# A spectral filter and two token MLPs on one core: the first layers of three units ahead of the first second layer

## The chip, the cores and the metric

The kernel runs on one core of a Trainium2 chip. The metric is the device time of one execution in microseconds; below, a time is a median of several runs where it says so, and the profile is one execution of its own. The engines are named as in the profile: PE (TensorE), DVE (VectorE), ACT (ScalarE), POOL (GpSimd) and SP, which here only issues transfers.

## What is computed

The input is `x`, four sequences of 3136 tokens of 256 numbers, in fp32.

```python
X = np.fft.rfft(x, axis=1)                       # a filter along the sequence
y = np.fft.irfft(X * (filt_r + 1j * filt_i), n=3136, axis=1)

u = y + np.real(np.fft.fft(np.fft.fft(y, axis=1), axis=2))   # mixing over both axes
un = (u - mean(u)) / np.sqrt(var(u) + 1e-6)
u = u + np.maximum(un @ w_ch1, 0.0) @ w_ch2      # first layer: weights 1a, 2a

xn = (u - mean(u)) / np.sqrt(var(u) + 1e-6) * g_ln
out = u + np.maximum(xn @ v_ch1, 0.0) @ v_ch2    # second layer: weights 1b, 2b
```

Means and variances are taken over the 256 numbers of a token; `w_ch1` and `v_ch1` have 256 x 1024 numbers, the other two 1024 x 256. The weights are in float64.

## The kernel before

**Transforms.** The sequence of 3136 is split as 64 x 49. For each of the four sequences `b`, `over_p(b)` does the transform over 64 and writes its result `g` to DRAM; `over_q(b)` reads it back, does the transform over 49, the filter and the way back, and writes the rows `v` to DRAM and a part `zt` to SBUF. For `b = 0` this is the opening of the program, up to some 85 us; for the others the generators are called in small turns in between the work of the MLPs. Of `over_p(1)`, ten turns run in the opening and six are put into steps by the table `P1`; `over_q(1)` is put into steps by `MID`, `OPQ` and `PAIRS`.

**Units.** The tokens are cut into 25 units of 512 (the last has 256). A unit is prepared by `prep_ticks(U)` in eight turns: two build `zs` and split the loaded rows `vr` into a high and a low half; two make the tokens `u` (26 matmuls, L216 and L549; ACT copies one half to `uo`, DVE adds and subtracts, L554 and L556); one takes statistics (`bs`, `mv`, `rs`, with a power on POOL at L598); one normalizes into four tiles `xn` (DVE L602); two transpose on PE (L611) and split into `xth` (ACT) and `xtl` (DVE, L220). For the second layer `ln_ticks(U, 1)` does the last four turns again, with L614 for the low half. Tables (`PREP1`, `PREPS`, `PREPN`, `LN0`, `LN`) say in which steps the turns stand.

**Steps.** A layer of a unit is a block of eight steps. Each step `m` has a w1 product of six matmuls of 512 columns (L682, into PSUM), from which ACT makes `hh` (L687) and DVE the low half `hl` (L688), and a w2 product (L705) of eight matmuls with `hh` and four with `hl`, 256 columns each. In the program's order the w1 product of step i + 1 stands ahead of all that is put into step i, and the w2 product of step i behind it. All numbers are split in a high and a low half, so that three passes give fp32. In this kernel the blocks follow each other as unit 0 first layer, unit 1 first, unit 0 second, unit 2 first, unit 1 second, and so on; the order is written out by hand, each engine runs its instructions in that order.

**Conversion of the weights.** Four weights of 4 chunks each, 16 in all, come as float64 words and are turned into a high and a low fp32 half by integer work. `conv_ticks` does it in ticks, as a pipeline: a full tick has, for the newest chunk, three DVE instructions on the words (L665 to L667), for the chunk before two ACT instructions (L658, L659), for the one before that two on DVE (L651, L653) and a product on POOL (L655), and for the oldest the split: the high half on ACT (L219) and the difference on POOL (L220). Three chunks of 1a are done in the opening (`NA`); the 13 others are run by the letters `c` of `DURING` and `AFTER` and then, one tick a step, by the steps in `CONV`: here 0, 1, 3, 6, 9, 11, 12, 14, 15, 17 and 19. On DVE a full tick is thus five instructions in a row, and one that is put into a step stands between two `hl`.

**The turn into the steps.** `AFTER` is a string that is run when `over_q(0)` is done: `p` is a turn of unit 0's preparation, `f` one of `over_p(1)`, `c` one of the conversion and `s` a split of constants. Unit 0's rows are read back from DRAM in this stretch.

## Time and profile before

| | us |
|---|---|
| median of 3 runs | 1429.06 |
| lowest and highest | 1428.6, 1431.17 |
| the profiled execution, its own time | 1427.74 |
| its span in the profile | 1425.9 |
| PE busy in it | 1384.6 |
| DVE, ACT, POOL busy in it | 885.6, 622.7, 408.3 |

A row of a timeline gives the start in us from the span's beginning, the length, the engine, the line and the tiles as out<-in; the number in brackets is how long the engine had stood idle ahead of it, and what it was waiting for. In a table of stretches an engine's number is its busy time in that stretch, with the number of its instructions. The granted clock (PEclk) is a share of full speed; 1.00 is 2.4 GHz and 0.50 is 1.2 GHz. Work of a line by groups: how many, busy time in all, mean of one in ns.

### The profile page before, as it was taken

To read this page: it belongs to the slowest core of one execution; us is meant where nothing else is said; L and a number is where in the kernel's file an instruction comes from. 1 tells how busy PE (TensorE), PEld (TensorE's weight loads), DVE (VectorE), ACT (ScalarE), POOL (GpSimd) and SP (SyncE) were. 2 spreads that over 40 slices of the span, in tenths; PEclk is the share of its full clock that TensorE was granted. 3 is DMA by queue.
4 is the path that set the end of the run, shared out by engine and by line. 5 is a ranking of instruction groups with operands and counts; after the bars stand their busy time and mean duration, and the time that the engine had idled before them with its cause. 6 is when DMAs were issued, how large, how long until landed. Compare 5 with 4: busy or idle time off the path is not lost.

```text
span 1425.9 us, 22918 instructions
## 1 busy us (share of the span) xinstructions
PE 1384.6 (97%) x8835; PEld 1221.6 (86%) x8835; DVE 885.6 (62%) x1814; ACT 622.7 (44%) x1350; POOL 408.3 (29%) x361
## 2 busy tenths in 40 slices
PE   4978999999999999999999999999999999999998
PEld 2437899888989999898999998898999999999998
DVE  2779977777554775767545666667555555555453
ACT  4755545645444544545344355445333233323222
POOL 1635534535231333434032244334100010100000
PEclk7988999999999999999999999999999999999999
DMA  9973332422233313312233233131000000000000
GB/s 325 316 272 108 102 99 83 141 78 85 77 115 124 97 49 114 109 48 68 68 103 118 77 90 114 42 114 62 19 30 30 31 1 31 30 15 16 30 15 23
DMA packets 65981, 123.66 MB, mean 87 GB/s; under 512 B 6096, under 2 KB 32848, under 8 KB 65872
## 3 DMA queue, kind: packets, MB, share of 16 engines
q1 hardware_dynamic: 49920, 99.00, 21.6%
q10 hardware_dynamic: 15952, 23.20, 5.0%
q8 instruction: 69, 1.13, 0.3%
q14 instruction: 40, 0.33, 0.1%
HBM read 83.12 MB, written 39.06 MB: 86 GB/s over the span
## 4 chain that ended last, share of the span: by engine, by line
PE 88%; DVE 5%; DMA 1%; issue 1%; ACT 0%; POOL 0%; ACTq 0%; POOLq 0%; DVEq 0%
PE ps L705 37%; PE ps L682 36%; PE ps L216 11%; PE ps L611 3%; DMA vd<-vst 1%; PE ps L439 1%; DVE we L651 1%; DVE wm L653 0%; DVE hl L688 0%; DVE wm L666 0%; DVE ww L667 0%; DVE xn L602 0%; PE ps L549 0%; POOL rs L598 0%; PE ps L302 0%
## 5 line engine op out<-in xcount | busy, mean ns | idle before, releaser
L687 ACT ACTIVATE hh<-ps 128x512 fp32r<-128x512 f32 (+1 forms) x400 | 235.4, 589 | 689.3 <-PE ps L682 666.9
L688 DVE SCALAR_TENSOR_TENSOR hl<-ps,hh 128x512 fp32r<-128x512 f32 (+1 forms) x400 | 271.7, 680 | 424.5 <-ACT hh L687 423.3
L682 PE MATMUL ps<-xth,w1a 128*128 128x512 f32 (+1 forms) x800 | 247.0, 391 | 0.0
L682 PE MATMUL ps<-xth,w1b 128*128 128x512 f32 (+1 forms) x800 | 243.7, 386 | 0.0
L705 PE MATMUL ps<-w2a,hh 128*128 128x256 f32 x1568 | 221.3, 283 | 2.0 <-ACT hh L687 2.0
L705 PE MATMUL ps<-w2b,hh 128*128 128x256 f32 x1568 | 218.3, 281 | 0.0
L705 PEld LDWEIGHTS ps<-w2b,hh 128*128 128x128 f32 x1568 | 206.2, 188 | 10.5
L705 PEld LDWEIGHTS ps<-w2a,hh 128*128 128x128 f32 x1568 | 205.3, 189 | 10.9 <-ACT hh L687 2.4
L598 POOL TENSOR_TENSOR rs<-rs,mhalf 128x4 f32<-128x4 f32 (+1 forms) x51 | 50.4, 988 | 413.8 <-DVE rs L597 405.6
L682 PE MATMUL ps<-xtl,w1a 128*128 128x512 f32 (+1 forms) x400 | 156.4, 391 | 0.0
L682 PE MATMUL ps<-xtl,w1b 128*128 128x512 f32 (+1 forms) x400 | 155.7, 389 | 0.0
L682 PEld LDWEIGHTS ps<-xth,w1a 128*128 128x128 f32 x800 | 136.8, 190 | 18.0 <-ACT xth L219 0.5
L682 PEld LDWEIGHTS ps<-xth,w1b 128*128 128x128 f32 x800 | 135.2, 188 | 16.5
L705 PE MATMUL ps<-w2a,hl 128*128 128x256 f32 x784 | 123.4, 279 | 3.8 <-DVE hl L688 3.8
L705 PE MATMUL ps<-w2b,hl 128*128 128x256 f32 x784 | 122.0, 277 | 0.1
L422 POOL TENSOR_TENSOR y<-y,t 128x512 f32<-128x512 f32 (+1 forms) x67 | 87.2, 1302 | 99.8 <-DVE t L420 85.7
L705 PEld LDWEIGHTS ps<-w2a,hl 128*128 128x128 f32 x784 | 104.9, 189 | 4.3 <-DVE hl L688 4.3
L705 PEld LDWEIGHTS ps<-w2b,hl 128*128 128x128 f32 x784 | 103.9, 188 | 0.3 <-DVE hl L688 0.3
L220 POOL TENSOR_TENSOR sl<-gr,sh 98x512 fp32r<-98x512 f32 x48 | 63.3, 1318 | 109.7 <-ACT sh L219 107.8
L220 POOL TENSOR_TENSOR sl<-y,sh 128x512 fp32r<-128x512 f32 (+1 forms) x51 | 67.2, 1317 | 79.9 <-issue 59.1
L682 PEld LDWEIGHTS ps<-xtl,w1a 128*128 128x128 f32 x400 | 75.8, 190 | 15.1
L682 PEld LDWEIGHTS ps<-xtl,w1b 128*128 128x128 f32 x400 | 75.3, 188 | 14.4
(115 smaller groups left out, 2040.6 us busy)
## 6 DMA issues: line engine op xcount, KB each, us to landing
fc<-in_ff SPq DMA_DIRECT2D x61, 512.0 KB
vd<-vst ACTq DMA_DIRECT2D x64, 200.0 KB
gr<-gd SPq DMA_DIRECT2D x64, 196.0 KB
xr<-in_x SPq DMA_DIRECT2D x48, 256.0 KB
vr<-vd SPq DMA_DIRECT2D x48, 256.0 KB
out<-u SPq DMA_DIRECT2D x24, 512.0 KB
gd<-gst ACTq DMA_DIRECT2D x28, 256.0 KB
gd<-gst SPq DMA_DIRECT2D x20, 256.0 KB
```

The costliest lines, as they stand in the source:

```text
L216: nc.tensor.matmul(out=o, lhsT=lhs[a], rhs=rhs[b], start=start and i == 0, stop=stop and i == 2)
L220: (lo_eng or nc.vector).tensor_tensor(out=lo, in0=src, in1=f32(hi), op=ALU.subtract)
L422: (nc.gpsimd if b or t < n - 1 else nc.vector).tensor_tensor(out=y[:, :nk], in0=y[:, :nk], in1=t2[:, :nk], op=ALU.add)
L439: nc.tensor.transpose(zp[:, a].rearrange("p t k -> p (t k)"), z[:, a], ident)
L598: nc.gpsimd.tensor_tensor(out=rs[:, tl], in0=rs[:, tl], in1=mhalf[:, tl], op=ALU.pow)
L611: nc.tensor.transpose(ps[:, t * 128:t * 128 + 128], xs[t][:, k * 128:k * 128 + 128], ident)
L651: nc.vector.scalar_tensor_tensor(out=p, in0=w[:, :, 1], scalar=-0x80000000, in1=p, op0=ALU.bitwise_and, op1=ALU.bitwise_or)
L682: nc.tensor.matmul(out=ps[:, :n], lhsT=w[:, a, k, m * 128:m * 128 + 128], rhs=xt[s][:, k, :n], start=i == 0, stop=i == 5)
L687: nc.scalar.activation(out=h[:, :n], in_=ps[:, :n], func=ACTF.Relu)
L688: nc.vector.scalar_tensor_tensor(out=l[:, :n], in0=ps[:, :n], scalar=0.0, in1=f32(h[:, :n]), op0=ALU.max, op1=ALU.subtract)
L705: nc.tensor.matmul(out=o[:, t % 2], lhsT=a[:, t * 128:t * 128 + 128], rhs=w[:, b, m], start=m == 0 and i == 0 and t % 2 == 0, stop=m == 7 ...
```

## The change

The blocks now begin with the first layers of units 0, 1 and 2 (24 steps), then the second layers of units 0 and 1, and from there on alternate as before. So unit 2's first layer is in steps 16 to 23 instead of 24 to 31 and is prepared by `PREP1` in steps 8 to 14; unit 3 has a table of its own (`PREP3`). The second layers' normalizations are counted back from the block that needs them. The chunks are converted in another order: of 1a and 1b those that the first four w1 products need come first, and the first chunk of 2a ahead of the last of 1a; the assertion in `w1_step` asks only for the two chunks that a product reads. One `c` leaves `AFTER`: the one ahead of the two turns that make unit 0's tokens; another turn of `over_p(1)` moves between unit 0's two transposing turns. The conversion takes steps 0, 1, 3, 5, 8, 10, 12, 14, 16, 18, 20 and 22; the six turns of `over_p(1)` steps 4, 7, 9, 11, 13 and 15; `over_q(1)` starts four steps later and gets one more pair of steps in 16.

```diff
+CHUNKS = {"1": (0, 1024, 512, 1536), "2": (0, 512, 1024, 1536)}
-AFTER = "ppcfspfcppfpfppfpppc"
-CONV = (0, 1, 3, 6, 9, 11, 12, 14, 15, 17, 19, 20, 21, 22, 23, 24, 25, 26, 27, 28)
-P1 = (2, 3, 4, 5, 7, 8, 9, 10, 10)
-OPQ = (2, 4)
-MID = 16
+AFTER = "ppcfspfppfpfpfpppc"
+CONV = (0, 1, 3, 5, 8, 10, 12, 14, 16, 18, 20, 22, 26, 27, 28)
+P1 = (4, 7, 9, 11, 13, 15, 17, 19, 20)
+OPQ = (3, 5)
+MID = 20
+PREP3 = (2, 3, 10, 11, 11, 12, 13, 14)
-LN0 = (8, 10, 12, 12)
-LN = (12, 13, 16, 19)
+LN0 = (-12, -9, -7, -5)
+LN = (-12, -11, -8, -5)
...
-            chunks += [(words, n, a) for a in range(0, 2048, 512)]
+            chunks += [(words, n, a) for a in CHUNKS[n[0]]]
         chunks = chunks[first:last]
+        if first:
+            chunks[:2] = chunks[1::-1]
...
-                conv_done.add((names[(i + first) // 4], (i + first) % 4))
+                conv_done.add((name, a // 512))
...
-        assert all(("1" + "ab"[layer], j) in conv_done for j in range(4)), (U, layer, m)
+        assert all(("1" + "ab"[layer], j + m // 4) in conv_done for j in (0, 2)), (U, layer, m)
...
-        blocks = [(0, 0)]
-        for U in range(1, NU + 1):
+        blocks = [(0, 0), (1, 0), (2, 0), (0, 1), (1, 1)]
+        for U in range(3, NU + 1):
             blocks += [(U, 0), (U - 1, 1)]
...
-                for w in (PREPS if V % 6 else PREPN) if U else PREP1:
+                if V == 3:
+                    s = index[V, 0] - 16
+                for w in PREP1 if V < 3 else PREP3 if V == 3 else PREPS if V % 6 else PREPN:
                     put(s + w, it)
...
-                call(s + 1 + new if U else -1, load_v, V)
+                call(s + 1 + new if V > 2 else s - 1, load_v, V)
...
-                e = index[U + 1, 0]
-                for w in [s + v for v in LN] if U else [e - 8 + w for w in LN0]:
-                    put(w, it)
+                for w in LN if U else LN0:
+                    put(index[U, 1] + w, it)
...
-            for each in range(1, len(PAIRS) + 1):
+            pr = PAIRS + [(7, 9)] if b == 1 else PAIRS
+            for each in range(1, len(pr) + 1):
```

Line numbers of the changed kernel are two to seven higher than those of the kernel before (L651 becomes L655, L688 becomes L692).

**DVE, from the loading of unit 0's rows to its normalization.** Before: the last instruction of one tick, a whole tick, then the sum `u`.

```order
L667 TENSOR_SCALAR ww<-ww 128x512
L651 SCALAR_TENSOR_TENSOR we<-ww,we 128x512
L653 SCALAR_TENSOR_TENSOR we<-ww,we 128x512
L665 TENSOR_SCALAR we<-ww 128x512
L666 TENSOR_SCALAR we<-ww 128x512
L667 TENSOR_SCALAR ww<-ww 128x512
L554 TENSOR_TENSOR u<-ps,uo 128x256
L556 TENSOR_TENSOR u<-ps,uo 128x256
L594 BN_STATS bs<-u 128x6 x2
```

The same place now:

```order
L671 TENSOR_SCALAR ww<-ww 128x512
L556 TENSOR_TENSOR u<-ps,uo 128x256
L558 TENSOR_TENSOR u<-ps,uo 128x256
L596 BN_STATS bs<-u 128x6 x2
L598 BN_AGGR mv<-bs 128x2 x2
```

The tick between the two is gone from here.

**DVE, unit 1's normalization in steps 4 to 6.** Before: `xn`, an `hl`, the low half `xtl` of the transposed tokens, then a tick.

```order
L597 TENSOR_SCALAR rs<-mv 128x4
L688 SCALAR_TENSOR_TENSOR hl<-ps,hh 128x512
L602 TENSOR_SCALAR xn<-u,mv,rs 128x256 x4
L688 SCALAR_TENSOR_TENSOR hl<-ps,hh 128x512
L220 TENSOR_TENSOR xtl<-ps,xth 128x512 x2
L651 SCALAR_TENSOR_TENSOR we<-ww,we 128x512
L653 SCALAR_TENSOR_TENSOR wm<-ww,wm 128x512
```

The same place now:

```order
L599 TENSOR_SCALAR rs<-mv 128x4
L692 SCALAR_TENSOR_TENSOR hl<-ps,hh 128x512
L604 TENSOR_SCALAR xn<-u,mv,rs 128x256 x4
L655 SCALAR_TENSOR_TENSOR we<-ww,we 128x512
L657 SCALAR_TENSOR_TENSOR wm<-ww,wm 128x512
L669 TENSOR_SCALAR we<-ww 128x512
L670 TENSOR_SCALAR wm<-ww 128x512
L671 TENSOR_SCALAR ww<-ww 128x512
L692 SCALAR_TENSOR_TENSOR hl<-ps,hh 128x512
L222 TENSOR_TENSOR xtl<-ps,xth 128x512 x2
```

The tick of step 5 stands between `xn` and `xtl`.

**DVE, unit 2's statistics and normalization.** Before (in steps 16 to 19, for a layer that begins in step 24):

```order
L594 BN_STATS bs<-u 128x6 x4
L596 BN_AGGR mv<-bs 128x2 x4
L597 TENSOR_SCALAR rs<-mv 128x4
L688 SCALAR_TENSOR_TENSOR hl<-ps,hh 128x512
L602 TENSOR_SCALAR xn<-u,mv,rs 128x256 x4
```

The same place now (in steps 12 and 13, for a layer that begins in step 16); the second set of statistics is unit 0's for its second layer.

```order
L596 BN_STATS bs<-u 128x6 x4
L598 BN_AGGR mv<-bs 128x2 x4
L599 TENSOR_SCALAR rs<-mv 128x4
L596 BN_STATS bs<-u 128x6 x4
L598 BN_AGGR mv<-bs 128x2 x4
L599 TENSOR_SCALAR rs<-mv 128x4
L655 SCALAR_TENSOR_TENSOR we<-ww,we 128x512
L657 SCALAR_TENSOR_TENSOR wm<-ww,wm 128x512
L669 TENSOR_SCALAR we<-ww 128x512
L670 TENSOR_SCALAR wm<-ww 128x512
L671 TENSOR_SCALAR ww<-ww 128x512
L692 SCALAR_TENSOR_TENSOR hl<-ps,hh 128x512
```

The four `xn` of unit 2 follow that `hl`.

## Rows read from the trace of the kernel before

**Rows 1.** The page, busy time of the engines over the span.

```profile
PE 1384.6 (97%) x8835; PEld 1221.6 (86%) x8835; DVE 885.6 (62%) x1814; ACT 622.7 (44%) x1350; POOL 408.3 (29%) x361
```

**Rows 2.** Table of stretches: length, then PE, PEld, DVE, ACT, POOL busy, clock, DMA.

```profile
93.00:109.00 16.00, 9.79 (x28) 6.35 (x29) 13.60 (x31) 5.93 (x12) 5.25 (x6) 0.79 0.62 220
109.00:142.60 33.60, 28.48 (x165) 25.04 (x165) 30.96 (x49) 18.45 (x38) 20.35 (x18) 0.90 0.31 101
142.60:173.00 30.40, 27.22 (x177) 24.16 (x176) 29.60 (x52) 16.38 (x33) 17.59 (x13) 0.99 0.36 114
173.00:198.00 25.00, 24.89 (x167) 22.57 (x166) 22.91 (x51) 10.55 (x20) 11.82 (x10) 1.00 0.13 41
198.00:400.00 202.00, 202.00 (x1317) 181.35 (x1316) 134.53 (x271) 105.53 (x243) 83.93 (x71) 1.00 0.33 102
```

**Rows 3.** Timeline of PE, the four longest waits from 95 us on.

```profile
100.93 0.56 PE L611 MATMUL ps<-ctail,xn 128*128 128x128 f32 x2 [3.94 <-DVE xn L602]
...
119.64 1.22 PE L705 MATMUL ps<-w2a,hl 128*128 128x256 f32 x4 [2.58 <-DVE hl L688]
...
138.71 0.30 PE L611 MATMUL ps<-ctail,xn 128*128 128x128 f32 x1 [2.21 <-DVE xn L602]
...
170.43 1.19 PE L705 MATMUL ps<-w2a,hh 128*128 128x256 f32 x8 [2.01 <-ACT hh L687]
```

**Rows 4.** Table of stretches again, one stretch of half clock.

```profile
119.20:122.40 3.20, 2.76 (x9) 2.38 (x10) 3.20 (x6) 1.32 (x3) 1.37 (x2) 0.50 0.00 0
```

**Rows 5.** DVE from 93 to 178 us by line, the five instructions of a tick.

```profile
L651 DVE SCALAR_TENSOR_TENSOR we<-ww,we 128x512 int32<-128x512 int32 x11 | 13.1, 1189 | 0.0
...
L666 DVE TENSOR_SCALAR wm<-ww 128x512 int32<-128x512 int32 x9 | 11.4, 1269 | 0.0
L667 DVE TENSOR_SCALAR ww<-ww 128x512 int32<-128x512 int32 x11 | 10.2, 929 | 0.0
L653 DVE SCALAR_TENSOR_TENSOR wm<-ww,wm 128x512 f32<-128x512 int32 x7 | 7.0, 994 | 0.0
...
L665 DVE TENSOR_SCALAR we<-ww 128x512 int32<-128x512 int32 x10 | 5.3, 527 | 0.0
```

**Rows 6.** Timelines of DVE and POOL: the longest tick and the shortest.

```profile
113.22 0.67 DVE L651 SCALAR_TENSOR_TENSOR we<-ww,we 128x512 int32<-128x512 int32 x1
...
114.23 1.63 POOL L220 TENSOR_TENSOR w2a<-we,w2a 128x512 fp32r<-128x512 f32 x1
...
114.62 1.53 DVE L665 TENSOR_SCALAR we<-ww 128x512 int32<-128x512 int32 x1
...
118.91 0.68 DVE L688 SCALAR_TENSOR_TENSOR hl<-ps,hh 128x512 fp32r<-128x512 f32 x1
...
161.78 0.67 DVE L651 SCALAR_TENSOR_TENSOR we<-ww,we 128x512 int32<-128x512 int32 x1
...
164.00 0.67 DVE L688 SCALAR_TENSOR_TENSOR hl<-ps,hh 128x512 fp32r<-128x512 f32 x1
```

**Rows 7.** Timeline of all engines around unit 0's sum.

```profile
93.34 1.78 DVE L651 SCALAR_TENSOR_TENSOR we<-ww,we 128x512 int32<-128x512 int32 x1
94.02 0.38 ACT L553 ACTIVATE uo<-ps 128x256 f32<-128x256 f32 x1 [0.59 <-PE ps L302]
...
97.72 0.41 DVE L554 TENSOR_TENSOR u<-ps,uo 128x256 f32<-128x256 f32 x1
```

**Rows 8.** Timeline of DVE, unit 1's normalization and the second low half.

```profile
137.22 2.72 DVE L602 TENSOR_SCALAR xn<-u,mv,rs 128x256 f32<-128x256 f32 x4 [0.53 <-POOL rs L598]
...
141.99 0.69 DVE L220 TENSOR_TENSOR xtl<-ps,xth 128x512 fp32r<-128x512 f32 x1 [0.16 <-ACT xth L219]
```

**Rows 9.** The chain that ended last: one w1 and one w2 product at full pace.

```profile
190.00 1.40 PE ps L682 x6
191.40 1.39 PE ps L705 x12
```

**Rows 10.** Timeline of DVE, the statistics of one unit.

```profile
182.05 1.39 DVE L594 BATCH_NORM_STATS2 bs<-u 128x6 f32<-128x256 f32 x4
```

More of the change, by code (lines that the diff above doesn't have):

```diff
@@ L850, in spectral_mlp_kernel @@
             if U < NU:
-                e = index[U + 1, 0]
-                for w in [s + v for v in LN] if U else [e - 8 + w for w in LN0]:
-                    put(w, it)
+                for w in LN if U else LN0:
+                    put(index[U, 1] + w, it)
             else:
                 for w in (9, 10, 12, 13):
-                    put(s + w, it)
+                    put(index[U, 0] + w, it)
         conv_at = CONV[:16 - NA + LAG + 1 - nc_]
@@ L875, in spectral_mlp_kernel @@
                 put(w, q)
-            for each in range(1, len(PAIRS) + 1):
+            pr = PAIRS + [(7, 9)] if b == 1 else PAIRS
+            for each in range(1, len(pr) + 1):
                 slots = []
                 for base in range(-8, end, 16):
-                    for h in sorted(PAIRS[:each]):
+                    for h in sorted(pr[:each]):
                         if base + h[0] > mid + (4 if b > 1 else OPQ[1] + 1) and base + h[1] < end:
```

## The prediction

> **What bounds the kernel now.** I read the page first: PE is busy for 97% of the span [rows 1], so only the rest can be won. The stage table says where the rest lies: from 198 us to 400 us PE is busy 202.00 of 202.00 us, while from 93 to 173 us it lacks 16.00 - 9.79, 33.60 - 28.48 and 30.40 - 27.22, that is 6.2 + 5.1 + 3.2 = 14.5 us [rows 2]. In the same three stages DVE is busy 13.60 of 16.00, 30.96 of 33.60 and 29.60 of 30.40 us. So in the opening DVE sets the pace, and afterwards PE does. Third, PE's timeline names the waits: 3.94 us for `xn` of unit 0, 2.58 us for an `hl`, 2.21 us for `xn` of unit 1, 2.01 us for an `hh` [rows 3]. All are DVE results, except the last, where ACT stood behind a conversion. After a wait PE also ran at half its clock for a while: granted clock 0.50, the 1.2 GHz level, from 119.2 to 122.4 us [rows 4], just behind the 2.58 us wait.
>
> What fills DVE is the conversion of the weights. One tick of it is five DVE instructions. Its means are 1.19 + 0.99 + 0.53 + 1.27 + 0.93 = 4.9 us [rows 5]; rows overlap by some 0.1 us each, so I take 4.4 us from start to start. The shortest runs from 161.78 to 164.00, 2.2 us; the longest from 113.22 to 118.91, 5.7 us [rows 6]. The long one has its L665 at 1.53 us while POOL runs the 1.63 us final difference of another chunk. So the spread is DVE and POOL standing in each other's way.
>
> **The change part by part.** I count up to the moment at which the w1 product of step 24 begins. By then both kernels have given PE the same matrix products (24 steps, the preparations of units 1 and 2, the rest of transform b = 1, unit 0's second normalization) and DVE the same list. Behind it PE is never late before, so a difference there is a difference at the end.
>
> *The start.* The tick between the landing of unit 0's last rows and their sum goes away. Before, `uo` is there at 94.02 + 0.38 = 94.4 us but `u` starts at 97.72, since DVE is in a tick that began at 93.34 [rows 7]. So 97.72 - 94.4 = 3.3 us come off the way to unit 0's first w1 product.
>
> *Up to unit 1.* That gain can't be kept, as I read the order. Between 93 us and the low half of unit 1's transposed tokens DVE has five full ticks before (one at 93.34, one ahead of step 0, three in steps 0, 1 and 3), and five after (one ahead of step 0, four in steps 0, 1, 3 and 5). DVE was idle only (16.00 - 13.60) + (33.60 - 30.96) = 5.0 us there [rows 2]. After, it waits for `uo` (1.0 us, since the tick that filled this time is gone), for `rs`, for the two `xth` and for the second `uo` of unit 1; by the order I make that 5 us as well. So `xtl` of unit 1 comes where it came, 142.0 + 0.7 us [rows 8]. The fourth tick of the steps now stands between `xn` and `xtl` of unit 1, where before there were 141.99 - (137.22 + 2.72) = 2.1 us [rows 8]; PE finds the tokens normalized some 4 us earlier and then waits as long for their low half. Meanwhile it has done less: three of the 512-column groups of transform b = 1 are still to come. Such a group is three matmuls; six of that width take 1.40 us [rows 9], so three groups are 2.1 us. On the other side the half clock that PE had there before falls into time in which it waits anyway; one such stretch of 3.2 us [rows 4] is worth 1.6 us. Together +0.5 us.
>
> *Unit 2.* Before, unit 2's first layer comes in step 24 and its preparation has room; unit 0's second layer, in step 16, was ready long ahead. After, unit 2 is due in step 16 and is prepared as tightly as unit 1. For unit 1 PE waited 2.21 us [rows 3]. For unit 2 the chain between sum and `xn` has, besides the tick, a second set of statistics, unit 0's. Its first four instructions take 1.39 us together [rows 10], the small ones behind them a little more; I put the set at 1.7 us. That makes 2.2 + 1.7 = +3.9 us. In return the waits of the stage from 142.6 to 173 us, 3.2 us [rows 2], came of ticks in steps 11, 12, 14 and 15; after, no two neighbouring steps hold a tick. I let all of it go: -3.2. Together +0.7 us.
>
> *Steps 16 to 24.* A tick stands right behind `xtl` of unit 2: 4.4 us, and 0.6 for the `hl` behind it [rows 6], make 5.0. PE has from there the rest of one w1 product and 1.39 + 1.40 + 0.9 us, 4.4 in all [rows 9]: +0.6 us. The second tick after it comes with DVE still behind, and I add another 0.5: +1.1 us. Before, PE lost 25.00 - 24.89 = 0.1 us in that stage [rows 2].
>
> *At nothing.* The exchanged order of two weight loads, the other order of w1's chunks and the new loads' places in SP's queue: each load still has over one step. SP holds nothing between the last stores of v and unit 0's row loads that it did not hold before. What covers the second half chunk of w2a is thin: its last difference on POOL comes about as late as the `hl` of its step; if it is later, PE waits up to one POOL operation, 1.6 us [rows 6].
>
> **The sum.** +0.5 + 0.7 + 1.1 = +2.3 us. The profiled execution would go from 1427.74 to 1430.0; it lies 1.3 us under the median, and against the median the forecast is 1429.06 + 2.3 = 1431.4 us. The unknown is the length of a tick, between 2.2 and 5.7 us [rows 6], ten of which count; I take 4.4, the mean. At 3.3 (the tick's own product on POOL in the way, nothing else) 5.5 us would come off in front of unit 1, more than the 3.3 us of the start; at 5.0, six more would be added in ten ticks, about half of it beside PE's work.
>
> **A rule of the Trainium skill.** What the rows show: L665 took 1.53 us beside a POOL difference against 0.53 us on the mean [rows 5, 6], while `hl`, which reads PSUM, took 0.67 to 0.68 us in either place [rows 6]. The Trainium skill, page "SBUF — State Buffer", section "🔬 SBUF: two separate sides", says that VectorE and GpSimd share one pair of ports under an exclusive lock, held for a whole instruction, when the VectorE one runs in a two-port mode or reads two SBUF inputs. By that rule, with which the trace agrees, a tick can't be spread out of its own collisions: it brings its own product and its own final difference to POOL, and each blocks one of the five. The sum by the rule stays as it is; if the collisions were chance, wider spacing would bring ticks near 2.2 us and the first rival would hold.
>
> **The rivals.** *Faster, 1425.0.* Conversion ticks stand on even steps and those of transform b = 1 on odd ones. If this keeps POOL's `sl` differences out of the ticks, a tick costs 3.3 us; the 3.3 of the start are kept but for the 0.5, unit 2's wait shrinks by 1.1, and the last stage's +1.1 goes: -2.8 - 0.4 + 0 = -3.2, and with half-rate stretches gone, another 1: -4.2. For it: PE's waits before are all within reach of a few us of DVE time. Against it: the tick between `xn` and `xtl`. Chance 0.28.
>
> *Slower, 1434.5.* PE's waits for unit 1's `xtl` and unit 2's `xn` grow together, and the granted clock falls behind each, as it did behind the 2.58 us wait. Each stretch at 0.50 costs at least half of 3.2 us [rows 4]; two that are not covered give +3.2 on top of +2.3. It decides from the point where the wait ahead of unit 2's transposes exceeds 3 us. For it: DVE is busy above 90% through these stages. Against: late DVE work also hides a slow PE. Chance 0.28.
>
> *Slower by another way, 1432.5.* The second batch's pointwise stage must go through its 18 turns in the steps from 28 on, not from 24 on. From 198 to 400 us DVE is at 134.53 of 202.00, POOL at 83.93 [rows 2]; a tenth more still fits. Were each turn to hold PE up by 0.06 us, 1.1 us would come on top of 2.3: 1432.5. Chance 0.04.
>
> **How the numbers follow.** The measurement can tell about 0.2%, 2.9 us, from no change. The forecast, 1431.4, lies within (chance 0.40, with the case that gains and losses cancel altogether). Faster is the first rival, 0.28; slower the two others, 0.32. The range from 1424.0 to 1436.0 holds both rivals' times and leaves out, below, ticks near 2.2 us, and above, ticks of 5 us and more with uncovered half clock.
>
> **What would show it.** DVE: `u` right behind `uo`, at about 94.5 us, and w1 of unit 0 beginning near 102 us instead of 106. Then PE waits at three places: the first `hl` of unit 0, `xtl` of unit 1 (about 3 us, at 139 to 143 us), `xn` of unit 2 (about 4 us, near 170). If the second and third are missing, the forecast is wrong to the fast side; if the granted clock shows half rate behind them with nothing else late, to the slow side. Ticks' mean length from the five DVE lines decides between the cases. PE waits after 210 us would speak for the last rival.

## The result, and the profile of the changed kernel

The changed kernel takes 1438.34 us (median of 6 runs, 1437.44 to 1443.55) against 1429.26 us for the kernel before, timed beside it (6 runs, 1428.47 to 1431.44). The ratio is 1.0073, 95% interval 1.0058 to 1.0088: slower by some 9 to 10 us, where 2.3 us were forecast, and outside the range. The profiled execution took 1437.44 us, its span is 1435.6 us, 9.7 us over the span of before.

PE's busy time over the span grew by 3 us only, and DVE's and POOL's by 1 us each [rows 1]:

```profile
PE 1387.6 (97%) x8835; PEld 1221.6 (85%) x8835; DVE 886.5 (62%) x1814; ACT 623.1 (43%) x1350; POOL 409.6 (29%) x361
```

So the work is nearly the same and the rest is waiting. The table of stretches says where (length, then PE, PEld, DVE, ACT, POOL busy, granted clock, DMA; the first four are the stretches of [rows 2]):

```profile
93.00:109.00 16.00, 10.92 (x44) 6.55 (x42) 12.23 (x26) 7.68 (x17) 5.83 (x6) 1.00 0.74 243
109.00:142.60 33.60, 24.71 (x135) 21.32 (x136) 28.90 (x49) 13.45 (x26) 18.21 (x13) 0.88 0.16 59
142.60:173.00 30.40, 28.49 (x181) 25.89 (x181) 25.37 (x53) 16.01 (x32) 15.72 (x13) 0.97 0.31 105
173.00:198.00 25.00, 21.65 (x131) 18.98 (x130) 23.78 (x38) 10.80 (x20) 11.91 (x9) 0.93 0.30 98
...
250.00:300.00 50.00, 48.81 (x305) 41.94 (x304) 38.38 (x75) 29.22 (x67) 25.85 (x21) 1.00 0.37 119
```

From 93 to 109 us PE does more than before (10.92 against 9.79 us). From 109 to 142.6 us it does 3.8 us less, from 173 to 198 us 3.2 us less, and there is a loss between 250 and 300 us, where before had none. PE's granted clock has fallen no further: its mean over the span is 0.989, against 0.988 before. PE's timeline names the waits (start, length, and in brackets the idle time ahead and what was waited for):

```profile
99.13 0.56 PE L613 MATMUL ps<-ctail,xn 128*128 128x128 f32 x2 [0.75 <-DVE xn L604]
101.68 0.65 PE L613 MATMUL ps<-ctail,xn 128*128 128x128 f32 x2 [1.99 <-DVE xn L604]
110.22 1.14 PE L709 MATMUL ps<-w2a,hl 128*128 128x256 f32 x4 [2.19 <-DVE hl L692]
118.28 0.73 PE L709 MATMUL ps<-w2a,hh 128*128 128x256 f32 x4 [1.64 <-ACT w2a L221]
120.99 1.22 PE L709 MATMUL ps<-w2a,hh 128*128 128x256 f32 x4 [1.97 <-POOL w2a L222]
138.55 0.33 PE L613 MATMUL ps<-ctail,xn 128*128 128x128 f32 x1 [2.15 <-DVE xn L604]
139.82 0.33 PE L613 MATMUL ps<-ctail,xn 128*128 128x128 f32 x1 [0.94 <-DVE xn L604]
141.12 1.65 PE L613 MATMUL ps<-ctail,xn 128*128 128x128 f32 x6 [0.97 <-DVE xn L604]
158.88 0.73 PE L709 MATMUL ps<-w2a,hl 128*128 128x256 f32 x4 [1.91 <-DVE hl L692]
...
177.07 0.98 PE L613 MATMUL ps<-ctail,xn 128*128 128x128 f32 x3 [3.35 <-DVE xn L604]
...
255.65 0.98 PE L613 MATMUL ps<-ctail,xn 128*128 128x128 f32 x3 [0.82 <-DVE xn L604]
```

Against [rows 3]: the wait for unit 0's `xn` fell from 3.94 to 0.75 us, the `hh` wait of 2.01 us is gone. New are two waits for `w2a` (1.64 and 1.97 us), one for unit 2's `xn` (3.35 us) and one for unit 3's (0.82 us); unit 1's `xn` now holds PE up three times, 4.06 us together, for one wait of 2.21 us and a short one.

**PE's lost time.** Waits alone leave out the half clock behind them. So for the rest of this text I take from each trace the spacing of PE's matmuls, subtract for each kind of matmul (its line, its shape, and those of the next) the median spacing of that kind in the kernel before, and add up what is left over by steps. "Lead" is the time from the first matmul with unit 0's landed rows (L302 before) to the first w1 product. us:

| kernel | lead | steps 0–7 | 8–15 | 16–23 | 24–79 |
|---|---|---|---|---|---|
| before | 12.6 | 10.9 | 4.3 | 0.6 | 1.4 |
| after | 8.7 | 16.9 | 7.7 | 0.6 | 4.2 |
| difference | −3.9 | +6.0 | +3.4 | 0 | +2.8 |

The differences add up to 8.3 us. The rows landed 1.4 us later in the execution of after (94.68 us against 93.28; in the other profiles below between 92.30 and 96.22, whatever the kernel). Together that is the 9.7 us between the spans. From step 76 on the two traces run in parallel.

Each row is read from one execution, and that sets how finely it can be read: `after_swap` and `after_mended` below run the same program up to step 24 and differ by 1.9 us in steps 0 to 7. The row of `tick_later` adds up to 3.9 us less than that of before, and the times of the two show no difference. So a cell that differs by under 2 us is not relied on by itself; the last column, 1.4 to 2.2 us or 4.0 to 4.3 us in every run, is steadier.

### The profile page after: what moved, and what is told of

It is laid out like the page before. It is cut to its first block, busy times and chain, and to the rows that moved or that the text cites. A ratio compares the mean times of both kernels' runs of the same rounds, so it can differ in the third digit from the quotient of the medians.

```text
span 1435.6 us, 22916 instructions
## 1 busy us (share of the span) xinstructions
PE 1387.6 (97%) x8835; PEld 1221.6 (85%) x8835; DVE 886.5 (62%) x1814; ACT 623.1 (43%) x1350; POOL 409.6 (29%) x361
## 4 chain that ended last, share of the span: by engine, by line
PE 90%; DMA 3%; DVE 3%; ACT 1%; issue 1%; POOL 1%; SPq 0%; ACTq 0%; POOLq 0%; DVEq 0%
PE ps L709 37%; PE ps L686 36%; PE ps L218 11%; PE ps L613 3%; DMA vd<-vst 2%; PE ps L304 1%; PE ps L441 1%; DMA xr<-in_x 1%; DVE xn L604 0%; DMA gd<-gst 0%; ACT gst L334 0%; PE ps L551 0%; PE ps L410 0%; DMA vr<-vd 0%; DVE we L655 0%
## 5 line engine op out<-in xcount | busy, mean ns | idle before, releaser
L692 DVE SCALAR_TENSOR_TENSOR hl<-ps,hh 128x512 fp32r<-128x512 f32 (+1 forms) x400 | 271.7, 679 | 435.4 <-ACT hh L691 434.5
L709 PEld LDWEIGHTS ps<-w2b,hh 128*128 128x128 f32 x1568 | 206.0, 188 | 10.2
L604 DVE TENSOR_SCALAR xn<-u,mv,rs 128x256 f32<-128x256 f32 x196 | 83.4, 485 | 11.1 <-POOL rs L600 7.8
```

What stands on the lines that cost most here:

```text
L604: nc.vector.tensor_scalar(out=xs[t], in0=u[:, t], scalar1=mv[:, t, 0:1], scalar2=rs[:, t:t + 1], op0=ALU.subtract, op1=ALU.mult)
L692: nc.vector.scalar_tensor_tensor(out=l[:, :n], in0=ps[:, :n], scalar=0.0, in1=f32(h[:, :n]), op0=ALU.max, op1=ALU.subtract)
L709: nc.tensor.matmul(out=o[:, t % 2], lhsT=a[:, t * 128:t * 128 + 128], rhs=w[:, b, m], start=m == 0 and i == 0 and t % 2 == 0, stop=m == 7 ...
```

## The experiments

Each kernel was timed beside the kernel before; the ratio is to that, with its 95% interval, and the columns behind it are those of the table above.

| kernel | time, us | ratio | lead | steps 0–7 | 8–15 | 16–23 | 24–79 |
|---|---|---|---|---|---|---|---|
| old_start | 1435.97 | 1.0059 (1.0044–1.0075) | 12.8 | 12.9 | 7.6 | 0.8 | 4.3 |
| only_tick | 1440.02 | 1.0085 (1.0070–1.0099) | 10.0 | 19.1 | 5.9 | 5.3 | 1.4 |
| ticks_moved | 1442.38 | 1.0102 (1.0086–1.0117) | 10.0 | 17.8 | 6.1 | 5.2 | 4.3 |
| product_dve | 1429.15 | 1.0004 (0.9996–1.0013) | 11.1 | 10.9 | 5.2 | 1.7 | 1.4 |
| blocks_only | 1435.94 | 1.0064 (1.0049–1.0078) | 12.0 | 10.2 | 9.7 | 1.0 | 4.0 |
| tables_only | 1428.94 | 1.0004 (0.9995–1.0012) | 12.2 | 12.9 | 2.7 | 0.2 | 1.9 |
| chunk_order | 1438.31 | 1.0072 (1.0059–1.0085) | 8.9 | 17.6 | 6.3 | 6.6 | 1.4 |
| tick_later | 1427.00 | 1.0004 (0.9992–1.0015) | 10.3 | 9.2 | 4.7 | 0.3 | 1.4 |
| ln0_late | 1436.99 | 1.0066 (1.0053–1.0079) | 12.6 | 10.4 | 7.3 | 4.7 | 4.0 |
| prep3_early | 1433.71 | 1.0041 (1.0028–1.0054) | 12.9 | 10.1 | 9.7 | 1.1 | 1.5 |
| after_extra | 1441.45 | 1.0095 (1.0080–1.0109) | 10.0 | 18.6 | 10.1 | 0.2 | 4.2 |
| mix1 | 1426.39 | 0.9986 (0.9974–0.9998) | 9.8 | 11.5 | 2.4 | 0.3 | 1.9 |
| after_swap | 1437.68 | 1.0055 (1.0039–1.0071) | 9.4 | 16.0 | 10.5 | 0.2 | 4.3 |
| after_mended | 1433.85 | 1.0036 (1.0023–1.0050) | 9.3 | 14.1 | 10.6 | 0.2 | 2.2 |
| mix2 | 1449.90 | 1.0148 (1.0130–1.0166) | 9.5 | 16.2 | 3.1 | 22.0 | 1.9 |
| mix3 | 1426.28 | 0.9993 (0.9982–1.0004) | 10.3 | 10.1 | 3.1 | 1.4 | 1.4 |

### The tick that was taken away, apart from the rest

`only_tick` is the kernel before with the new `AFTER`; `old_start` is the changed kernel with the old one.

```diff
-AFTER = "ppcfspfcppfpfppfpppc"
+AFTER = "ppcfspfppfpfpfpppc"
```

> The kernel before with the new string AFTER alone: the conversion tick leaves the stretch between the landing of unit 0's rows and their sum, blocks, chunk order and all other tables as before (the steps of CONV then hold one tick more, the last in step 20). Theory of positions (what costs is a tick that stands inside the chain of a unit that is due at once): the sum starts 3.3 us earlier, but the following ticks come later by one step each; 1427 to 1431 us, no clear difference. Rival, order of the blocks (the new order of blocks alone costs the 9 us): the 3.3 us of the start are kept, 1425 to 1427 us. Rival, late chunks of 2a: PE waits 1 to 4 us for the halves of 2a in steps 1 to 6 and the kernel is slower, 1430 to 1434 us.

> The changed kernel with the old string AFTER: the tick is back between landing and sum, so all ticks in steps come one earlier; blocks, chunk order and tables as changed. Theory of positions: unit 1's and unit 2's chains still have their ticks in steps 5 and 12, so within 2 us of the changed kernel's 1438.3. Rival, order of the blocks: the same 1438 or up to 3.3 us slower, 1441, as the start is lost. Rival, late chunks of 2a: the waits of 1.64 and 1.97 us for a half of 2a go, and with them up to 4 us: 1434 to 1436.

Alone, taking the tick away costs the kernel before 11 to 12 us, more than any of the three expectations said; the third had the cause right, and put the waits at 1 to 4 us. Its PE timeline:

```profile
112.51 0.74 PE L705 MATMUL ps<-w2a,hh 128*128 128x256 f32 x4 [2.66 <-ACT w2a L219]
118.60 1.22 PE L705 MATMUL ps<-w2a,hh 128*128 128x256 f32 x4 [5.35 <-POOL w2a L220]
127.51 0.72 PE L705 MATMUL ps<-w2a,hh 128*128 128x256 f32 x4 [0.89 <-POOL w2a L220]
```

PE comes earlier and then waits 8.9 us for halves of 2a's chunks (and 1.25 us more at 148.74 us). old_start came out as its third expectation said. Put back into the changed kernel, the tick lengthens the lead by 4.1 us and takes 4.0 us out of steps 0 to 7, and with it the two `w2a` waits; the intervals of after and old_start overlap, so of the 2.4 us between their medians I say only that the tick's removal gained nothing. The larger part of the loss, 7 to 8 us in old_start, is not in the tick.

### Why the chunk is late: POOL, and then one tick too few

In the changed kernel POOL and DVE stand like this in steps 0 to 2 (timelines of the two engines, first DVE, then POOL):

```profile
111.95 0.69 DVE L655 SCALAR_TENSOR_TENSOR we<-ww,we 128x512 int32<-128x512 int32 x1
112.55 0.69 DVE L657 SCALAR_TENSOR_TENSOR we<-ww,we 128x512 f32<-128x512 int32 x1
113.15 0.43 DVE L669 TENSOR_SCALAR we<-ww 128x512 int32<-128x512 int32 x1
113.48 0.43 DVE L670 TENSOR_SCALAR wm<-ww 128x512 int32<-128x512 int32 x1
113.82 0.43 DVE L671 TENSOR_SCALAR ww<-ww 128x512 int32<-128x512 int32 x1
```

```profile
112.17 2.34 POOL L535 CAST zmid<-zsl 1x256 fp32r<-1x256 f32 x1 [2.35 <-DVE zsl L520]
114.59 1.31 POOL L222 TENSOR_TENSOR w1a<-we,w1a 128x512 fp32r<-128x512 f32 x1
115.85 1.72 POOL L659 TENSOR_TENSOR we<-we 128x512 f32<-128x512 f32 x1
117.53 1.73 POOL L222 TENSOR_TENSOR sl<-vr,sh 128x512 fp32r<-128x512 f32 x1
119.22 1.72 POOL L222 TENSOR_TENSOR w2a<-we,w2a 128x512 fp32r<-128x512 f32 x1
```

From 112 us POOL has no gap; the half of 2a's second chunk that PE needs in step 2 is its fifth piece of work and ends at 120.94 us, where PE has stood since 119.02. On DVE that third tick takes 6.5 us, from 116.37 to 122.91. In the kernel before the same difference is the row at 114.23 us of [rows 6]: with the tick in front done, this chunk is finished by the second tick behind the tokens, now by the third.

Three runs asked whether the order of the chunks, or a tick more, can mend that. `chunk_order` is only_tick with the change's order of the chunks, `after_extra` the changed kernel with one more tick, in step 2, and `after_swap` the changed kernel with 2a's second chunk ahead of 1a's last, which is needed only in step 4:

```diff
-CONV = (0, 1, 3, 5, 8, 10,
+CONV = (0, 1, 2, 3, 5, 8, 10,
...
-            chunks[:2] = chunks[1::-1]
+            chunks[:3] = [chunks[1], chunks[2], chunks[0]]
```

> The kernel before with the new AFTER (no tick between the landing and the sum) and the new order of the chunks, in which 2a's first chunk goes ahead of 1a's last; blocks and the other tables as before. only_tick, which differs by the order of the chunks alone, took 1440.0 us. If its loss came from 2a's chunks being late (waits of 2.7, 5.4, 0.9 and 1.3 us for w2a in its trace), most of those waits go and the time is 1429 to 1433 us. If it came from the tick's work falling on DVE later, whatever chunk it is, the time stays at 1438 to 1441 us with the waits on hl or xn instead.

> The changed kernel with one more conversion tick, in step 2: CONV = (0, 1, 2, 3, 5, 8, ...). Every chunk from the third tick on comes as early as with the tick in front. Theory (the waits of 1.64 and 1.97 us for w2a at 118 and 121 us come of each chunk being one tick later than before): at least the second goes, the loss in steps 0 to 4 falls from 9.9 to 6 or 7 us, time 1435 to 1437 us. Rival (DVE's and POOL's work as such is late, whichever chunk): PE waits as long, for hl or w2a, and xn of unit 1 comes later by a tick: 1438 to 1441 us.

> The changed kernel with 2a's second chunk converted ahead of 1a's last one (needed only in step 4): the third tick behind the tokens then finishes 1a's last chunk, the second 2a's second. Theory (one late chunk): the waits of 1.64 and 1.97 us for w2a in step 2 go, 3 us and more come off steps 0 to 4, the time falls to 1434.5 to 1436 us. Rival (ticks and POOL as such): another wait for hl or w2a stands in their place and the time stays at 1437 to 1440 us.

None of the three mended it, and the times are those of the expectations' second branches, or 0.5 us above them (after_extra). In chunk_order the waits for `w2a` still come to 3.20, 1.96 and 1.25 us. In after_extra PE waits longer, not shorter: the added tick stands behind the third one and can't hasten it, so this run was badly aimed. Its 10.1 us in steps 8 to 15 are not the added tick's either: after_swap, which has no such tick, loses 10.5 us there. In after_swap step 2 runs free, and PE stands in step 4, for the chunk that was put off:

```profile
121.39 0.65 PE L686 MATMUL ps<-xth,w1a 128*128 128x512 f32 x1 [2.06 <-POOL w1a L222]
```

Steps 0 to 3 lose 4.5 us less and steps 4 to 7 3.6 us more. So it is not one chunk in the wrong place: with a tick less in front, the third tick's chunk was late in each of the orders tried, whichever chunk that was.

`mix2` shows the same debt further on. It is the kernel before with the new `AFTER`, the new order of the chunks with that exchange, and the thinner tables:

> The kernel before, with its order of blocks, and of the change the AFTER without the tick, the sparser tables (fourth tick in step 6) and the order of the chunks, with 2a's second chunk ahead of 1a's last as in after_swap. If the start's gain can be kept once no chunk is late: 1423 to 1426 us, under mix1 (1426.4). If the work of the tick that is missing in front is missed later in any case: 1427 us or more.

It is 21 us slower. The waits of PE from 174 to 230 us (us in total, times, longest):

```profile
PE ps L708 <- POOL w2b L221: 9.6, 4, 4.3
PE ps L708 <- ACT w2b L220: 4.6, 4, 1.2
```

Unit 0's second layer begins in step 16 there and runs through 2b faster than the ticks deliver it. In the changed kernel the second layer begins in step 24, and nothing of the kind is seen. Nor is it in tables_only below, which has the old order of blocks and the thinner conversion, but also the tick: it loses 0.2 us in steps 16 to 23. So it takes the thinner conversion together with the missing tick to starve 2b this far in the old order of blocks; the new order has both and no such waits. By the ratios only_tick (+12 us), blocks_only (+9) and tables_only (0) therefore don't add up; the whole change is slower by 9 to 10.

### The order of the blocks against the tables

`blocks_only` is the kernel before with the part of the diff on `blocks`, `PREP3`, `LN0`, `LN` and `load_v`; `tables_only` has `CONV`, `P1`, `OPQ`, `MID` and the extra pair.

```diff
+PREP3 = (2, 3, 10, 11, 11, 12, 13, 14)
-LN0 = (8, 10, 12, 12)
-LN = (12, 13, 16, 19)
+LN0 = (-12, -9, -7, -5)
+LN = (-12, -11, -8, -5)
...
-        blocks = [(0, 0)]
-        for U in range(1, NU + 1):
+        blocks = [(0, 0), (1, 0), (2, 0), (0, 1), (1, 1)]
+        for U in range(3, NU + 1):
```

> The kernel before with the new order of blocks alone (units 0, 1 and 2 first, with PREP3, LN0, LN and the place of the v loads); AFTER, CONV, P1, MID, OPQ, PAIRS and the order of the chunks as before. Theory A (the order of blocks itself costs: three preparations in a row in front, the fourth unit prepared late because its buffer is held): the loss of the changed kernel in steps 4 to 16 and 32 to 52, some 5 to 7 us, is here too: 1434 to 1437 us. Rival B (the tables that thin out the conversion and push transform b = 1 and the second batch back are the cost): 1428 to 1431 us here, and the loss in tables_only. A sign either way: the wait for xn of unit 3 and unit 2 in the trace.

> The kernel before with the new CONV, P1, MID, OPQ and the extra pair (7,9) alone; blocks, AFTER and the order of the chunks as before. Theory A (order of blocks): no loss, 1427 to 1430 us, since the sparser conversion leaves DVE more room in steps 0 to 16. Rival B (tables): 1434 to 1437 us, with PE waiting for late chunks of 1b or for the second batch's pointwise stage.

Theory A held: the order of blocks alone costs as much as old_start, and the tables alone cost nothing. The loss has two places. One is unit 2's `xn` (PE, then DVE ahead of it):

```profile
174.32 2.30 PE L612 MATMUL ps<-ctail,xn 128*128 128x128 f32 x8 [6.03 <-DVE xn L603]
```

```profile
166.02 1.39 DVE L595 BATCH_NORM_STATS2 bs<-u 128x6 f32<-128x256 f32 x4
167.34 0.36 DVE L597 BATCH_NORM_AGGREGATE mv<-bs 128x2 f32<-128x6 f32 x4
167.73 0.17 DVE L598 TENSOR_SCALAR rs<-mv 128x4 f32<-128x4 f32 x1
167.81 1.40 DVE L595 BATCH_NORM_STATS2 bs<-u 128x6 f32<-128x256 f32 x4
...
169.60 0.69 DVE L652 SCALAR_TENSOR_TENSOR we<-ww,we 128x512 int32<-128x512 int32 x1
...
171.47 1.52 DVE L668 TENSOR_SCALAR ww<-ww 128x512 int32<-128x512 int32 x1
172.91 0.68 DVE L689 SCALAR_TENSOR_TENSOR hl<-ps,hh 128x512 fp32r<-128x512 f32 x1
173.51 1.72 DVE L603 TENSOR_SCALAR xn<-u,mv,rs 128x256 f32<-128x256 f32 x4
```

Between unit 2's statistics (done at 167.8) and its `xn` (173.5) stand unit 0's statistics, 1.8 us, a tick, 3.3 us, and an `hl`, 0.6 us. The other place is unit 3, below.

`ln0_late` takes unit 0's statistics out of this place:

```diff
-LN0 = (-12, -9, -7, -5)
+LN0 = (-7, -6, -5, -4)
```

> blocks_only with LN0 = (-7, -6, -5, -4) in place of (-12, -9, -7, -5): unit 0's second statistics, which stood on DVE between unit 2's statistics and its xn (166.0 to 169.6 us in the trace of blocks_only, with 1.4 + 0.4 + 0.2 = 1.8 us of them unit 0's), come after unit 2's tokens. Theory (the list of DVE between sum and xn sets PE's wait of 6.03 us for xn of unit 2): the wait falls to some 4 us, unit 0's second layer in step 24 is not late, time 1.5 to 2 us under that of blocks_only, 1434 us. Rival (the wait is set by something else, POOL's power or the rows): wait and time as in blocks_only.

The wait fell as expected, from 6.03 to 4.21 us:

```profile
174.13 2.30 PE L612 MATMUL ps<-ctail,xn 128*128 128x128 f32 x8 [4.21 <-DVE xn L603]
```

The time did not fall (1436.99 against 1435.94 us, where 1434 was expected). What steps 8 to 15 gained (2.4 us) steps 20 to 23 lost (3.8 us more), where PE now stood for unit 0's own `xn`, 0.43 and 0.88 us, and ran at half clock behind that. The list of DVE did set that wait, as expected; the gain in time did not come.

`ticks_moved` did the same to the ticks, in the changed kernel:

```diff
-CONV = (0, 1, 3, 5, 8, 10, 12, 14, 16,
+CONV = (0, 1, 3, 6, 8, 10, 14, 15, 16,
```

> The changed kernel with the ticks of steps 5, 12 and 14 in steps 6, 14 and 15, so that none stands between sum and low half of unit 1 and unit 2. Theory of positions: the waits for xn of unit 1 (2.15 + 0.94 + 0.97) and of unit 2 (3.35 us) shrink to under half, and some of the half clock with them: 1432 to 1435 us. Rival, order of the blocks: the chains stay late, since the same DVE work is due: 1437 to 1439 us. Rival, late chunks of 2a: those of the last chunk come one step later, 1438 to 1440 us.

The wait for unit 2's `xn` fell to 0.34 us, and yet this is the slower kernel by 4 us, above all three expectations; two of the three waits for unit 1's `xn` stayed (2.14 and 0.94 us). A wait of 1.25 us for `w2a` came at 142 us, and one of 2.46 us for an `hl` at 191.6 us. What the moved ticks freed in one place was paid for in another.

`prep3_early` prepares unit 3 one step earlier in blocks_only, and `after_mended` does that in after_swap:

```diff
-PREP3 = (2, 3, 10, 11, 11, 12, 13, 14)
+PREP3 = (2, 3, 9, 10, 10, 11, 12, 13)
```

> blocks_only with unit 3 prepared one step earlier: PREP3 = (2, 3, 9, 10, 10, 11, 12, 13). Theory: the losses of the trace of blocks_only around 254 to 263 us (PE waits for xn of unit 3 and, in the first step of unit 3, for xtl; 2.6 us over the kernel before in steps 32 to 52) are due to its preparation starting only when unit 0's buffer is free; one step (3.3 us) earlier takes away the wait in the first step of unit 3, 1 us and more: 1434 to 1435 us. Rival (DVE is too full there whichever step it is): the waits move with it and the time stays at 1436 us.

> after_swap with PREP3 = (2, 3, 9, 10, 10, 11, 12, 13). If the terms are independent: 2.2 us (the measured step from blocks_only to prep3_early) under after_swap, 1432 to 1434 us. If unit 3's wait was partly covered by what was late before, less.

Both held, prep3_early 0.3 us below its range. In blocks_only the stretch from 250 to 300 us has PE at 48.83 of 50 us; in prep3_early:

```profile
250.00:300.00 50.00, 50.00 (x325) 44.63 (x324) 37.46 (x75) 28.63 (x67) 23.79 (x20) 1.00 0.39 119
```

The loss behind step 24 goes from 4.0 to 1.5 us; it is 1.4 in the kernel before. after_mended is the best form of the changed kernel that was run, 5 us slower than before; unit 2 and the late third tick remain.

### What a tick costs DVE

`product_dve` is the kernel before with the tick's product on DVE in place of POOL.

```diff
-                nc.gpsimd.tensor_tensor(out=v, in0=v, in1=p.bitcast(F32), op=ALU.mult)
+                nc.vector.tensor_tensor(out=v, in0=v, in1=p.bitcast(F32), op=ALU.mult)
```

> The kernel before with the product of each conversion tick (L655) on DVE instead of POOL; nothing else changed. If a tick's length is made of collisions of DVE and POOL (4.4 us against 2.2 alone), the tick takes one DVE instruction of 0.6 us more and loses one collision of about 1.1 us: DVE is free some 5 us earlier in the opening, and of PE's 14.5 us of waits 2 to 5 us go: 1424 to 1427 us. If the ticks' length is something else, DVE has 13 times 0.6 us more and the kernel is slower, 1431 to 1435 us.

No difference in time, so neither expectation held: the collisions are real, but taking one out of the tick frees nothing. DVE by line, from 93 to 198 us (count, busy time, mean in ns):

```profile
L651 DVE SCALAR_TENSOR_TENSOR we<-ww,we 128x512 int32<-128x512 int32 x12 | 12.0, 996 | 0.0
...
L655 DVE TENSOR_TENSOR wm<-wm,we 128x512 f32<-128x512 f32 x9 | 8.2, 908 | 0.3
L665 DVE TENSOR_SCALAR we<-ww 128x512 int32<-128x512 int32 x10 | 7.5, 749 | 0.0
L666 DVE TENSOR_SCALAR wm<-ww 128x512 int32<-128x512 int32 x9 | 5.9, 657 | 0.0
L667 DVE TENSOR_SCALAR ww<-ww 128x512 int32<-128x512 int32 x11 | 4.8, 437 | 0.0
```

The product takes 0.91 us on DVE. Against the kernel before in the same stretch (nearly the means of [rows 5]) L666 falls from 1.27 to 0.66 us, L667 from 0.93 to 0.44 and L651 from 1.15 to 1.00, now that POOL's product no longer runs beside them; L665 grows from 0.53 to 0.75. DVE's busy time in the second and third stretch of [rows 2] stays where it was, 60.53 us against 30.96 + 29.60 = 60.56:

```profile
109.00:142.60 33.60, 28.01 (x162) 24.32 (x162) 31.95 (x54) 18.85 (x38) 15.86 (x14) 0.92 0.29 97
142.60:173.00 30.40, 26.41 (x171) 23.78 (x169) 28.58 (x54) 16.23 (x32) 10.72 (x9) 0.98 0.29 94
```

What the product costs DVE on POOL, by lengthening others, it cost here on DVE itself.

### Kernels that might beat both

`tick_later` keeps the tick but puts it behind unit 0's second normalized tile; `mix1` adds tables_only's thinner tables, with the fourth tick in step 6; `mix3` adds only the thinner conversion.

```diff
-AFTER = "ppcfspfcppfpfppfpppc"
+AFTER = "ppcfspfppfpcfppfpppc"
```

> The kernel before with the one tick moved within AFTER: from in front of the sum of unit 0's last rows to behind the second normalized tile, ahead of its transposes; nothing else. By the theory that a tick costs what it delays on the way to the first w1 product, u starts some 3 us earlier and the tick then delays the second xth and xtl by its length less the wait for the transposes: first w1 product 1 to 2 us earlier, time 1426 to 1429 us. By the rival that DVE's total work up to unit 1's xtl sets the pace, no difference: 1428 to 1430 us.

> What the runs so far point to as the best: the kernel before (its order of blocks) with the tick behind the second normalized tile (as tick_later), and tables_only's sparser conversion and transform b = 1, but the fourth tick of the steps in step 6. By the losses of the two runs apart (steps 4 to 8: 4.7 us in tick_later; steps 12 to 16: 1.9 us in tables_only against 4.7 in tick_later) it takes 2 to 3 us off: 1424 to 1426 us. By the rival, that a tick taken out of one stage comes back in the next, 1427 to 1429 us.

> tick_later with the thinner conversion alone, CONV = (0, 1, 3, 6, 8, 10, 12, 14, 16, ...); transform b = 1 and the second batch as before. If the thinner conversion is what lowers the loss in steps 8 to 16 (4.7 us in tick_later, 2.4 in mix1), this has 2 to 3 us there and keeps tick_later's 9.2 in steps 0 to 8 (11.5 in mix1): 1423.5 to 1426 us. If the thinner transform is what does it: 4 to 5 us in steps 8 to 16 and 1426 to 1429 us.

In tick_later the lead is 2.3 us shorter and its profile loses no more later, but the ratio shows no difference (0.9992 to 1.0015): 1 to 2 us are less than these runs can tell, with a landing of the rows that varies by 4 us from one profile to the next. mix1 is the only kernel here whose interval lies under 1: 1426.39 us, ratio 0.9986 (0.9974 to 0.9998), some 2 us, between its two expectations. With seventeen kernels timed, one interval that ends so close under 1 is a hint and does not show a gain. mix3 doesn't separate from the kernel before, and so what gives mix1 its smaller loss in steps 8 to 15 stays open: the conversion alone leaves 3.1 us there, with 1.4 us lost behind it, and these differences are within what one profile can tell.

## Why the prediction was wrong, point by point

The prediction's sum was +0.5 us up to unit 1, +0.7 at unit 2, +1.1 in steps 16 to 23 and nothing behind them, +2.3 us; the table has +2.1, +3.4, 0 and +2.8, together +8.3 us. Three of its steps failed: the half clock ahead of unit 1 that was to be covered (1.6 us), the sum at unit 2 (2.7 us), and the loss behind step 24 that was put at nothing (2.8 us). The w2a term, also put at nothing, had the path wrong.

**What bounds the kernel: right, with one exception.** Nearly all losses but the one of unit 3 lie between 93 and 205 us, and DVE's results end most of the waits. The two new waits for `w2a` end with ACT and POOL.

**The start: right, and a little small.** `u` begins at 95.91 us, right behind `uo`, as forecast:

```profile
95.91 0.42 DVE L556 TENSOR_TENSOR u<-ps,uo 128x256 f32<-128x256 f32 x1 [0.90 <-PE ps L304]
```

The lead is shorter by 3.9 us (forecast 3.3).

**Up to unit 1: the gain is eaten, as forecast, but by another path.** Forecast net +0.5 us, measured −3.9 + 6.0 = +2.1 us. The first w1 product of unit 1 begins 50.16 us after the rows landed (144.84 − 94.68), before 50.13 us (143.41 − 93.28). So the whole gain is gone, and the 2.1 us are the three groups of transform b = 1 that PE still owes: both as forecast. What failed in the sum is the return of 1.6 us for half clock. PE does not wait through that stretch, it works in it (length, PE busy, and the clock third from the end):

```profile
141.10:144.50 3.40, 3.38 (x16) 3.24 (x17) 3.40 (x8) 1.20 (x2) 1.83 (x1) 0.50 0.26 72
```

The path was another, too. The prediction had unit 1 normalized some 4 us earlier, with PE then waiting for `xtl`. But `xn` begins where it began, at 137.15 us against 137.22 [rows 8], though a tick less stands ahead of it. The rows landed 1.4 us later, and DVE stood idle 2.02 us for the `hh` ahead of the `hl` of step 4, at 125.60 us, whose w1 product comes on PE behind the `w2a` waits. PE's three waits came at 138 to 142 us, for `xn` and not for `xtl`: the four `xn` took 4.23 us, against 2.72 in [rows 8].

```profile
137.15 4.23 DVE L604 TENSOR_SCALAR xn<-u,mv,rs 128x256 f32<-128x256 f32 x4 [0.53 <-POOL rs L600]
```

Beside them POOL ran two `sl` differences, as before, and then one more, of a weight chunk, from 139.58 to 140.91 us. tables_only has the same three waits (2.15, 0.94 and 0.97 us), so they come of the tables and not of the order of blocks.

**"At nothing", the second half chunk of w2a: wrong.** The prediction named the thin cover and priced its loss at up to one POOL operation, 1.6 us, and then entered 0. It was 1.64 + 1.97 = 3.61 us. The row was there: in the kernel before that difference runs at 114.23 us with the second tick behind the tokens [rows 6], and a tick less in front pushes it to the third. I counted ticks on DVE and found five against five; the count that mattered was that of chunks finished when PE asks for each. In the time up to step 8 these waits don't come on top: old_start, which has none of them, loses as much (12.8 + 12.9 = 25.7 us, against 8.7 + 16.9 = 25.6). They ate the gain that I had given to DVE's list, so that part of the forecast came true partly by luck.

**Unit 2: the mechanism right, the sum wrong.** Forecast +3.9 − 3.2 = +0.7 us, measured +3.4. PE's wait for unit 2's `xn`, put at 3.9 us, was 3.35 us; the second set of statistics, put at 1.7 us, was worth 1.82 us in ln0_late (6.03 − 4.21). Two things were left out. The first is the half clock behind that wait: by the spacing of PE's matmuls step 15 loses 5.5 us, of which 3.35 are the wait; most of the rest is work at 0.50, from 178.6 us on (shown below). The second took back most of the return of 3.2 us. The waits of before in this stretch are indeed gone, but step 11 now loses 2.2 us, by a new wait of 1.91 us for the `hl` of step 10 behind a tick of 5.7 us that was put into step 8 (DVE, the tick's first row and that `hl`):

```profile
152.45 0.67 DVE L655 SCALAR_TENSOR_TENSOR we<-ww,we 128x512 int32<-128x512 int32 x1
...
158.15 0.68 DVE L692 SCALAR_TENSOR_TENSOR hl<-ps,hh 128x512 fp32r<-128x512 f32 x1
```

In step 8 unit 2's preparation begins as well, and POOL runs its `zmid` and its difference of `vr` beside that tick. In tables_only, where unit 2 is prepared eight steps later, the tick of step 8 takes 3.3 us (153.60 to 156.93) and no such wait is seen; in old_start, with both, it takes 5.7 us again and PE waits 1.91 us. So this loss belongs to neither part of the change alone. The term "no two neighbouring steps hold a tick" said nothing on how long a tick is.

**Steps 16 to 23: wrong to the other side.** +1.1 us forecast, 0 measured. The late tokens of unit 2 may have left DVE time to catch up; no run tests that.

**"Behind it PE is never late before": carried over to the changed kernel, and wrong there.** 2.8 us are lost, all but some 0.4 of them at unit 3. The sentence holds for the kernel before; but the change has a table for unit 3 that starts its sums as late as steps 34 and 35, and I priced no step of `PREP3`. In blocks_only, which loses as much there, prep3_early takes that loss away.

**The tick's length: right.** 4.4 us were taken; in after the means of the five add up to 4.6 us with their overlaps (93 to 198 us), 4.8 us before by the same count. From start to start the ten ticks take 4.1 us in the mean (2.2 to 6.5), 4.4 before. The Trainium skill, page "SBUF — State Buffer", section "🔬 SBUF: two separate sides", has VectorE and GpSimd under one exclusive lock for some instructions; what it gave for this case, that spreading ticks out doesn't free them of their own collisions, agrees with these two sums, and with the shorter rows of product_dve, in which one of the two collisions is taken out.

**The rivals.** The faster one fell with the tick's length. The slower one at 1434.5 us had its condition met: unit 2's wait is 3.35 us, over the 3 us named, and PE runs at half clock behind it, as behind the waits before (table of stretches, the clock is the third number from the end):

```profile
120.60:124.00 3.40, 3.01 (x11) 2.81 (x12) 2.98 (x4) 0.00 (x0) 1.76 (x2) 0.50 0.00 0
...
178.60:182.00 3.40, 3.40 (x16) 3.30 (x15) 2.96 (x4) 2.47 (x5) 1.30 (x1) 0.50 0.02 5
```

3.4 us at 0.50 are 1.7 us of work. But its sum did not hold: the half clock moved and did not grow. In the kernel before 6.6 us at 0.50 lay around the first w1 product (102.2 to 108.8 us), in the changed kernel 3.4 us lie behind it (110.3 to 113.7 us, at 0.51), and the mean granted clock over the span is 0.988 and 0.989. So the rival had the place right; what made the kernel slower is waiting, and the measured time lies 4 us above the rival's. The third, a denser second batch, is hardly seen: steps 60 to 79 lose 0.4 us more, as they do in tables_only, and the loss at unit 3 has its own cause.

**Left open.** Why after_swap and after_mended lose 10.5 us in steps 8 to 15, 3 us more than the changed kernel, was not followed up. The PE waits of after_swap in these steps are those of the changed kernel (1.91 and 3.36 us against 1.91 and 3.35), but the granted clock is lower:

```profile
142.60:173.00 30.40, 28.49 (x166) 25.23 (x166) 23.79 (x45) 15.43 (x31) 13.19 (x12) 0.90 0.30 98
```

0.90 against 0.97 in the changed kernel is 2.1 us of PE's work at the full clock. Behind the wait of 1.91 us PE runs at 0.50 from 159.1 to 162.5 us there, and at 1.00 behind the same wait in the changed kernel. What sets it lower wasn't tried.

## What to carry to other kernels

Where work is done in a pipeline of ticks ahead of its use, a tick taken from a place where it delays something isn't saved: list for each piece the tick that finishes it and the moment its reader asks, before and after, and price every piece whose tick moves behind its reader. Bringing three preparations in a row to the front needs room on the engine that makes them; when a wait goes, look at the next use of the same engine, since ln0_late, ticks_moved and after_swap only moved it. The parts of a change can meet: a tick and a preparation that were harmless apart stood in one step together, and the tick took 5.7 us instead of 3.3. A table for one unit deserves the same working as one for all: here one step in it was worth some 2.5 us.

## What the runs showed of the hardware

POOL's `zmid` from `zsl` took 2.34 us in the changed kernel, in the row at 112.17 us shown above, and 0.73 us in the kernel before:

```profile
113.42 0.73 POOL L533 CAST zmid<-zsl 1x256 fp32r<-1x256 f32 x1 [0.29 <-DVE zsl L518]
```

The long one lies under five DVE instructions that follow each other without a gap, each at its short time (0.69, 0.69, 0.43, 0.43, 0.43 us): the small POOL instruction ended 0.26 us after the last of them, at 114.51 us. It is no stray row, though spans on POOL are rough: in the profiles of the other runs the same cast took 2.33 or 2.34 us eleven more times, each time under five short DVE instructions of a tick. Where it took 0.72 or 0.73 us beside a tick, as in the row above, the tick's second instruction was lengthened instead, to 0.88 or 0.89 us. So in a collision it isn't always DVE that is lengthened, as in [rows 6]; a POOL instruction can lose against a whole run of them. The Trainium skill, page "SBUF — State Buffer", section "🔬 SBUF: two separate sides", says that whichever of the two starts first has the ports for its whole instruction. By that `zmid` would have waited for the one DVE instruction that it met; the 2.34 us disagree, unless the lock passes from one DVE instruction to the next, and no run here tells that apart. What decides between the two outcomes isn't shown either.
